# Token mixing of the first batch by groups of two head pairs instead of pair by pair, in a fused block-sparse attention and mixer kernel

## The chip, the core and the metric

The kernel runs on one core of a Trainium2 chip. A core has a matrix engine (TensorE, PE in the profile; its weight loads are shown apart as PEld), a vector engine (VectorE, DVE), a scalar engine (ScalarE, ACT), GpSimd (POOL) and SyncE (SP), each with its own program, and 16 DMA engines. Matmuls write to PSUM, and DVE or ACT bring the results to SBUF. The metric is the time of one execution on the device in microseconds, as a median of several; lower is better.

## The reference

Four batches, eight heads, 768 positions, 64 channels a head. Attention sees only some 32 x 32 blocks: the diagonal band, the first and last block row and column, and three sampled blocks for each block row. Its output, with the heads side by side as 512 channels, goes through a mixer: token mixing along the 768 positions, then channel mixing along the 512 channels.

```python
scores = scale * np.matmul(q, k.transpose(0, 1, 3, 2))          # mask: band, edges, sampled blocks
scores = np.where(mask, scores, -1000000000.0)
attn = np.exp(scores - max); attn = attn / (sum + 1e-09)
x = np.matmul(attn, v)              # then (batch, position, 8 heads * 64 channels)

xt = x.transpose(0, 2, 1)
h = np.maximum(xt @ w_tok1, 0.0) @ w_tok2     # 768 -> 256 -> 768, along positions
u = x + h.transpose(0, 2, 1)
h2 = np.maximum(u @ w_ch1, 0.0) @ w_ch2       # 512 -> 1536 -> 512, along channels
return u + h2
```

Token mixing treats each of the 512 channels by itself. So it can be done for any part of the channels as soon as the heads of that part are through attention. Channel mixing needs all 512 channels of a batch.

## The kernel before

The kernel works on 16 pairs of heads, four pairs to a batch. For each pair there are nine steps: a scores product on PE into a PSUM tile `ps`, an exponential on ACT into `et`, for later pairs a multiplication by the mask on DVE, and a product with V on PE into `po`, which DVE normalises into `x`. Token mixing takes `x` through `pm_tok` and `a_t`, adds to `x`, and transposes it into `uT`. Channel mixing (`pm_ch`, `rc`, `o`) reads `uT`.

All instructions are put in order when the program is built. A planner holds streams of PE instructions with priorities (the lower the number, the sooner) and lists of operations for the other engines, estimates when their inputs are ready, and at each step emits the first that is ready. Each engine then executes its instructions in the order in which they were emitted; the planner's estimates only shape this order.

```python
if self.now < self.tight:                      # the first 40 us of the plan
    t += 300.0 if 1.5 < s[0] < 2.5 else 100.0 if s[0] == 1 else 0.0
if t <= self.now: ... emit()
# ACT and DVE operations: of those that are ready, the one with the lowest (prio, number);
if eng == "act" and prio > 0 and self.exp_pending:
    continue                                   # ACT leaves other work while an exponential is due
```

The arrival of loads is an estimate as well. Loads are issued by GpSimd in the order V of pair 0; K, Q, V of pair 1; of pair 2; the two token weights; K, Q, V of pair 3; and so on.

```python
dma = {"free": 7.95 * US, "n": 0}
RATE = 200.0
LATE = (0, 290, 350, 0, 0, 190, 40, 700, 0)

def landing(issue, nbytes):
    late = LATE[dma["n"]] if dma["n"] < len(LATE) else 0
    dma["n"] += 1
    dma["free"] = max(dma["free"] + late, issue + 3.2 * US) + nbytes / RATE
    return Ev(dma["free"] + 0.15 * US)
```

K and Q of pairs 1 to 3 are transposed on PE straight from the landed rows, two slots of one head per transpose, without a relayout on DVE. This is so before and after the change:

```python
if raw is None:
    rows = lays[nm][:, c, :, :].rearrange("p h d -> p (h d)")       # pairs 4 to 7: after a relayout
else:
    lo = 2 * (c % 3)                                                 # pairs 1 to 3: the landed rows
    rows = raw[:, c // 3, lo : lo + 2, :].rearrange("p c d -> p (c d)")
```

Batches 1 to 3 do their token mixing by groups of two pairs (`tok`): products of 256 columns, and the transpose to `uT` by DMA. Batch 0 does it pair by pair (`tok_first`): products of 128 columns, and the transpose on PE. Its line numbers in the profile are L913 (first product), L936 (second), L945 (addition), L959 (transpose), L971 (copy); those of `tok` are L857, L882, L890.

```python
def tok_first(p):                              # p: pair 0 to 3 of batch 0
    g, lo = p // 2, 128 * (p % 2)
    urgent = 0.5 if p < 3 else -1
    deps = [x_there[p, h] for h in range(3)] + [tok1_there]
    # 2 x 6 matmuls: pm[128, 2, 128] += w_tok1 tile * x[:, g, sc, lo : lo + 128]
    # relu on DVE or ACT: a_t[:, :, 0:128] = max(pm, 0), priority `urgent`
    # twice: 6 matmuls into pm[128, 3, 128], then on DVE  x += pm  (128 x 384), priority `urgent`
    # 6 transposes of 128 x 128 into one PSUM tile, then one copy (128 x 768) to uT

P.stream(0, qk_stream())                       # scores
P.stream(1, pv_stream())                       # values
P.stream(TRP, tr_stream())                     # TRP = 2: transposes of K and Q
P.stream(TOKP, tok_first_stream(range(3)))     # TOKP = 0.7: token mixing of pairs 0 to 2
P.stream(-1, tok_first_stream((3,)))           # of pair 3, ahead of everything
P.stream(3, tok_stream((1, 2, 3)))             # of batches 1 to 3, by groups
P.stream(4, ch_stream())                       # channel mixing
```

Channel mixing goes over 12 x 2 tiles with four products each, one for each pair's part of `uT`, and the fourth needs pair 3 of the batch:

```python
yield 162.5, [st[b]["uT_there"][dmc], ch1_there[dmc]], tags, emit, ...   # dmc = 0 .. 3
```

Of the kernel before, what the change touches and what calls it, by code (L numbers as in the profile page):

```python
# [8 lines left out]
FP32 = mybir.dt.float32  # L9
BF16 = mybir.dt.bfloat16  # L10
# [4 lines left out]
ALU = mybir.AluOpType  # L15
# [159 lines left out]
def kernel(  # L175
# [12 lines left out]
    nc = tc.nc  # L188
# [3 lines left out]
    NC = 6  # L192
# [5 lines left out]
    NET = 7  # L198
    NPE = 8
    NT0 = 4  # L200
    TOKP = 0.7
    TRP = 2

    sb1 = ctx.enter_context(tc.tile_pool(name="sb1", bufs=1))
    sbw = ctx.enter_context(tc.tile_pool(name="sbw", bufs=2))
    psS = ctx.enter_context(tc.tile_pool(name="psS", bufs=2, space=bass.MemoryType.PSUM))
    psO = ctx.enter_context(tc.tile_pool(name="psO", bufs=1, space=bass.MemoryType.PSUM))
    psM = ctx.enter_context(tc.tile_pool(name="psM", bufs=3, space=bass.MemoryType.PSUM))
    ctx.enter_context(tc.manual_schedule())

    w_tok1 = sb1.tile([128, NC, DT], BF16, name="w_tok1")
    w_tok2 = sb1.tile([128, 2, 128, NC], BF16, name="w_tok2")
    w_ch1 = sb1.tile([128, 4, DC], BF16, name="w_ch1")
    w_ch2 = sb1.tile([128, 12, DM], BF16, name="w_ch2")
    ident = sb1.tile([128, 128], BF16, name="ident")
# [3 lines left out]
    P = Planner({"ps": 2, "po": 1, "pm": 3, "et": NET, "a_t": 2, "o": 3, "rc": 2,  # L219
                 "uT": 3})  # L220
    US = 1e3


    raws, arrive = {}, {}
    dma = {"free": 7.95 * US, "n": 0}
    RATE = 200.0
    LATE = (0, 290, 350, 0, 0, 190, 40, 700, 0)

    def landing(issue, nbytes):
        late = LATE[dma["n"]] if dma["n"] < len(LATE) else 0  # L230
        dma["n"] += 1
        dma["free"] = max(dma["free"] + late, issue + 3.2 * US) + nbytes / RATE
        return Ev(dma["free"] + 0.15 * US)


# [55 lines left out]
    tok1_there, tok2_raw = Ev(), Ev()  # L291
# [34 lines left out]
    for i in range(8):  # L326
# [5 lines left out]
        out=ind[R, :, :], in_=free(one[R, 0:1], 0, [[0, NC], [0, 128]]), compare_op=ALU.is_ge,  # L332
# [3 lines left out]
        out=ind[R, :, :], in_=ind[R, :, :], compare_op=ALU.is_ge, fill=0.0,  # L336
# [3 lines left out]
        out=ident[:, :], in_=free(one[:, 0:1], 0, [[0, 128]]), compare_op=ALU.is_equal, fill=0.0,  # L340
# [21 lines left out]
        out=edge[R, :], in0=edge[R, :], scalar1=-11.5, scalar2=None, op0=ALU.add  # L362
# [3 lines left out]
        out=edge[R, :], in0=edge[R, :], scalar1=121.0, scalar2=None, op0=ALU.is_gt  # L366
    )
    nc.vector.tensor_scalar(
        out=bandg[R, :], in0=dkf[R, :], scalar1=1.0, scalar2=edge[R, 0:1],
# [299 lines left out]
    def alias(a, b):  # L669
        a.same_as = b  # L670
# [4 lines left out]
    xs, x_there, po_of = {}, {}, {}  # L675
# [138 lines left out]
    def relu_op(o, i, deps, prio):  # L814
        n = i.free_size()

        def emit(eng):
            if eng == "act":
                nc.scalar.activation(out=o(), in_=i, func=AF.Relu)  # L819
            else:  # L820
                nc.vector.tensor_scalar(  # L821
                    out=o(), in0=i, scalar1=0.0, scalar2=None, op0=ALU.max
                )

        return P.op(("dve", "act"), {"dve": dve_psum(n), "act": act_cost(n)}, deps, emit, prio=prio)

    def new_uT(b):
        P.take("uT", st[b]["uT_rel"])
        st[b]["uT"] = sbw.tile([128, 2, NC, 2, 128], BF16, tag="uT", bufs=3, name=f"uT{b}")

    def turn_by_crossbar(b, g, u_evs):
        def emit(eng):
            if g == 0:
                new_uT(b)
            nc.sync.dma_start_transpose(
                out=st[b]["uT"][:, g, :, :, :].rearrange("e c m p -> e (c m) p"),
                in_=st[b]["u"][:, g, :, :].rearrange("p c e -> p (c e)"),
            )

        ev = P.op(("sp",), {"sp": 1600.0}, u_evs, emit, prio=2, lat=4000.0,  # L840
                  tags=[("uT", 1)] if g == 0 else [])
        for dmc in (2 * g, 2 * g + 1):
            alias(st[b]["uT_there"][dmc], ev)

    def tok(b, g):
        deps = [x_there[2 * g + 4 * b + i, h] for i in range(2) for h in range(3)] + [tok1_there]

        urgent = 3
        box = {}
        last, rel = Ev(), Ev()  # L850
        for t in range(2):
# [44 lines left out]
            alias(rel, ev)  # L896
            u_evs.append(ev)
        alias(a_rel, last)
        turn_by_crossbar(b, g, u_evs)

    def tok_first(p):
        g, lo = p // 2, 128 * (p % 2)
        urgent = 0.5 if p < 3 else -1
        box, last, rel = {}, Ev(), Ev()
        deps = [x_there[p, h] for h in range(3)] + [tok1_there]
        yield lambda: 0 in xs
        for t in range(2):
            for sc in range(NC):
                def emit(t=t, sc=sc):
                    if t == 0 and sc == 0:  # L910
                        P.take("pm", rel)
                        box["pm"] = psM.tile([128, 2, 128], FP32, tag="pm", name=f"pm_tok1_0_{p}")
                    nc.tensor.matmul(  # L913
                        out=box["pm"][:, t, :], lhsT=w_tok1[:, sc, 128 * t : 128 * t + 128],
                        rhs=xs[0][:, g, sc, lo : lo + 128],
                        start=(t == 0 and sc == 0), stop=(t == 1 and sc == NC - 1),
                    )
                begin = t == 0 and sc == 0
                yield 56.0, deps, [("pm", 1), ("a_t", 1)] if begin else [], emit, last if t == 1 and sc == NC - 1 else None
        if 0 not in st:  # L920
            st[0] = dict(u=xs[0], uT_there=[Ev() for _ in range(4)], uT_rel=Ev())
        a_rel = Ev()
        P.take("a_t", a_rel)
        a_t = sbw.tile([128, 2, 256], BF16, tag="a_t", name=f"a_t0_{p}")
        a_there = relu_op(lambda: a_t[:, :, 0:128], box["pm"][:, :, :], [last], urgent)
        alias(rel, a_there)
        u_evs = []
        for s3 in range(2):
            last, rel, ubox = Ev(), Ev(), {}
            for i in range(3):  # L930
                for t in range(2):
                    def emit(i=i, t=t, s3=s3, rel=rel, ubox=ubox):
                        if i == 0 and t == 0:
                            P.take("pm", rel)
                            ubox["pm"] = psM.tile([128, 3, 128], FP32, tag="pm", name=f"pm_tok2_0_{p}_{s3}")
                        nc.tensor.matmul(  # L936
                            out=ubox["pm"][:, i, :], lhsT=w_tok2[:, t, :, 3 * s3 + i],
                            rhs=a_t[:, t, 0:128], start=(i == 0 and t == 0), stop=(i == 2 and t == 1),
                        )
                    begin = i == 0 and t == 0  # L940
                    yield 56.0, [a_there, tok2_raw], [("pm", 1)] if begin else [], emit, last if i == 2 and t == 1 else None

            def add(eng, s3=s3, ubox=ubox):
                u = xs[0][:, g, 3 * s3 : 3 * s3 + 3, lo : lo + 128]
                nc.vector.tensor_tensor(out=u, in0=ubox["pm"][:, :, :], in1=u, op=ALU.add)  # L945

            ev = P.op(("dve",), {"dve": 556.0}, [last], add, prio=urgent)
            alias(rel, ev)
            u_evs.append(ev)
        alias(a_rel, last)  # L950
        last, rel, tbox = Ev(), Ev(), {}
        for sc in range(NC):
            def emit(sc=sc, rel=rel, tbox=tbox):
                if sc == 0:
                    if p == 0:
                        new_uT(0)
                    P.take("pm", rel)
                    tbox["pt"] = psM.tile([128, NC, 128], BF16, tag="pm", name=f"pm_ut_0_{p}")
                nc.tensor.matmul(  # L959
                    out=tbox["pt"][:, sc, :], lhsT=xs[0][:, g, sc, lo : lo + 128],  # L960
                    rhs=ident[:, :], start=(sc == 0), stop=(sc == NC - 1), is_transpose=True,
                )
            tags = [("pm", 1)] if sc == 0 else []
            if sc == 0 and p == 0:
                tags.append(("uT", 1))
            yield 56.0, [u_evs[sc // 3]], tags, emit, last if sc == NC - 1 else None

        def evac(eng, tbox=tbox):
            o, i = st[0]["uT"][:, g, :, p % 2, :], tbox["pt"][:, :, :]
            copy = nc.scalar.copy if eng == "act" else nc.vector.tensor_copy  # L970
            copy(out=o, in_=i)  # L971

        ev = P.op(("dve", "act"), {"dve": 555.0, "act": 740.0}, [last], evac, prio=urgent)
        alias(rel, ev)
        alias(st[0]["uT_there"][p], ev)

    def ch(b, pool, tag):
        yield lambda: b in st
# [77 lines left out]
    def tr_stream():  # L1056
        for p in range(NP):
            yield from transposes(p)

    def tok_stream(bs):  # L1060
        for b in bs:
            for g in range(2):
                yield from tok(b, g)

    def tok_first_stream(ps):
        for p in ps:
            yield from tok_first(p)

    def ch_stream():
        for b in range(B):  # L1070
            yield from ch(b, psM, "pm")

    P.stream(0, qk_stream())
    P.stream(1, pv_stream())
    P.stream(TRP, tr_stream())
    P.stream(TOKP, tok_first_stream(range(3)))
    P.stream(-1, tok_first_stream((3,)))
    P.stream(3, tok_stream((1, 2, 3)))
    P.stream(4, ch_stream())
    P.stream(1.8, mask_stream())  # L1080
# [78 lines left out]
```

## Time and profile before

| | before |
|---|---|
| time, median of 3 | 255.49 us (255.35 to 255.6) |
| span of the profiled execution | 253.6 us |
| PE busy | 246.9 us (97%), 2805 matmuls |
| PEld busy | 159.9 us (63%) |
| DVE busy | 179.4 us (71%) |
| ACT busy | 174.5 us (69%), 144 exponentials of 1022 ns |
| POOL busy | 49.5 us (20%) |
| first exponential starts, last starts | 7.4 us, 190.3 us |

All times within the profile count from the start of the span. A group of instructions is written as its line, engine, operation, output and inputs, shapes and count, then busy time and mean of one, then the idle time of the engine just before such instructions and what ended it. In the chain of waits each piece is work that the end of the program depended on. Matmuls are pipelined: the time that one takes from start to end is longer than the distance to the next, so runs of them show their rate better than single ones.

### The profile page before, as it was taken

The page shows a single profiled execution, that of the slowest core. Times are in us where ns is not written, and L with a number is a line of the kernel's source. Part 1 is how long each engine was busy: PE and PEld are TensorE (multiplying, and loading weights), DVE is VectorE, ACT ScalarE, POOL GpSimd, SP SyncE. Part 2 cuts the span into 40 slices and gives each one's busy share as a digit, 9 for nine tenths or more (in the row PEclk, how much of TensorE's full clock was granted, in tenths as well). Part 3 has the DMA queues.
Part 4 walks back from the last instruction along what each step waited for, and adds up shares of the span by engine and source line. Part 5 has one row for each costly group of instructions (what it writes and reads, how often), then busy time and mean ns, then how long its engine had stood idle before and what let it go on. Part 6 is the DMA issues. An engine that isn't in the chain of part 4 may idle for free.

```text
span 253.6 us, 6679 instructions
## 1 busy us (share of the span) xinstructions
PE 246.9 (97%) x2805; PEld 159.9 (63%) x2805; DVE 179.4 (71%) x394; ACT 174.5 (69%) x216; POOL 49.5 (20%) x84
## 2 busy tenths in 40 slices
PE   8889999999999999999999999999999999999994
PEld 3679998755666556656676566567567644566444
DVE  7784978998998988899889898988885312200222
ACT  5899999788888577778888777677786510277000
POOL 8746979477400000000000000000000000000000
PEclk9999999999999999999999999999999999999999
DMA  6999999999955926254032212311400212300122
GB/s 146 185 218 202 212 203 205 203 201 201 201 80 128 162 82 92 48 136 106 3 72 56 62 44 42 105 44 44 103 3 1 53 53 84 124 3 0 41 115 94
DMA packets 42462, 26.36 MB, mean 104 GB/s; under 512 B 23680, under 2 KB 38800, under 8 KB 42432
## 3 DMA queue, kind: packets, MB, share of 16 engines
q0 software_dynamic: 15104, 12.98, 32.4%
q1 hardware_dynamic: 27056, 12.76, 20.6%
q8 instruction: 22, 0.36, 0.6%
q10 hardware_dynamic: 272, 0.20, 0.3%
q14 instruction: 8, 0.07, 0.1%
HBM read 26.74 MB, written 6.29 MB: 130 GB/s over the span
## 4 chain that ended last, share of the span: by engine, by line
PE 92%; ACT 4%; DVE 2%; issue 1%
PE pm_ch L994 25%; PE pm_ch L1020 25%; PE ps L691 16%; PE po L777 14%; ACT et L701 3%; PE pm_tok L882 3%; PE pm_tok L857 3%; PE ps_idle L321 2%; PE pm_tok L913 1%; PE tk L633 1%; PE pm_tok L936 1%; PE tq L633 1%; DVE et L709 0%; DVE qtb L422 0%; DVE qtb L662 0%
## 5 line engine op out<-in xcount | busy, mean ns | idle before, releaser
L701 ACT ACTIVATE et<-ps 128x1024 bf16<-128x1024 f32 x144 | 139.2, 1022 | 32.1 <-PE ps L691 31.3
L994 PE MATMUL pm_ch<-uT,w_ch 128*128 128x384 bf16 x384 | 72.6, 326 | 0.1
L709 DVE TENSOR_TENSOR et<-et,mask 128x1024 bf16<-128x1024 bf16 x108 | 70.3, 683 | 1.2 <-ACT et L701 1.2
L1020 PE MATMUL pm_ch<-w_ch,rc 128*128 128x512 bf16 (+2 forms) x312 | 70.8, 363 | 0.0
L777 PEld LDWEIGHTS <-et 128*128 128x128 bf16 x1152 | 47.6, 97 | 16.5 <-issue 3.4
L691 PE MATMUL ps<-qtb,ktb 64*128 64x256 bf16 (+1 forms) x576 | 54.6, 272 | 2.2 <-ACT et L701 2.1
L777 PE MATMUL po<-vaug,et 128*128 128x65 bf16 x1152 | 54.3, 193 | 0.2 <-DVE et L709 0.2
L994 PEld LDWEIGHTS <-w_ch 128*128 128x128 bf16 x384 | 34.3, 97 | 20.7 <-issue 2.7
L819 ACT ACTIVATE rc<-pm_ch 128x384 bf16<-128x384 f32 x58 | 28.5, 492 | 24.3 <-PE pm_ch L994 24.2
L1032 DVE TENSOR_TENSOR o<-pm_ch,x 128x512 f32<-128x512 f32 x23 | 15.8, 688 | 41.5 <-PE pm_ch L1020 41.5
L1020 PEld LDWEIGHTS <-rc 128*128 128x128 bf16 x312 | 27.3, 97 | 24.4 <-issue 1.9
L691 PEld LDWEIGHTS <-ktb 64*128 64x128 bf16 (+1 forms) x576 | 29.0, 95 | 21.5 <-issue 16.7
L821 DVE TENSOR_SCALAR rc<-pm_ch 128x384 bf16<-128x384 f32 x38 | 21.1, 555 | 7.1 <-PE pm_ch L994 6.6
L792 DVE TENSOR_TENSOR x<-po,recip 128x256 bf16<-128x256 f32 x48 | 20.4, 424 | 1.7
L791 DVE RECIPROCAL recip<-po 128x4 f32<-128x4 f32 x48 | 8.6, 180 | 10.0 <-PE po L777 9.8
L890 DVE TENSOR_TENSOR x<-pm_tok,x 128x512 bf16<-128x512 f32 x18 | 11.8, 684 | 2.4 <-PE pm_tok L882 2.4
L882 PE MATMUL pm_tok<-a_t,w_tok 128*128 128x256 bf16 x72 | 10.0, 275 | 0.0
L857 PE MATMUL pm_tok<-x,w_tok 128*128 128x256 bf16 x72 | 9.2, 273 | 0.0
L882 PEld LDWEIGHTS <-w_tok 128*128 128x128 bf16 x72 | 7.5, 127 | 0.6 <-issue 0.2
L259 POOL DMA_DIRECT2D vraw<-in_v_dram x10 | 7.4, 737 | 2.3 <-DVE qtb L662 1.0
L537 POOL COPY mask<-maskb 128x240 bf16<-128x240 bf16 (+1 forms) x18 | 7.4, 491 | 0.0
L259 POOL DMA_DIRECT2D kraw<-in_k_dram x9 | 6.7, 742 | 3.8 <-PE pm_tok L913 1.4
(104 smaller groups left out, 133.9 us busy)
## 6 DMA issues: line engine op xcount, KB each, us to landing
out_dram<-o SPq DMA_DIRECT2D x23, 256.0 KB, 2.0
w_ch<-in_moe_w_ch_dram POOLq DMA_DIRECT2D x8, 384.0 KB, 10.2
vraw<-in_v_dram POOLq DMA_DIRECT2D x10, 192.0 KB, 7.6
kraw<-in_k_dram POOLq DMA_DIRECT2D x9, 192.0 KB, 8.2
qraw<-in_q_dram POOLq DMA_DIRECT2D x9, 192.0 KB, 7.8
w_tok<-in_moe_w_tok_dram POOLq DMA_DIRECT2D x2, 384.0 KB, 10.2
ktb<-in_v_dram POOLq DMA_DIRECT2D x3, 192.0 KB, 7.3
kf<-in_k_dram SPq DMA_DIRECT2D x2, 192.0 KB, 3.2
```

The source lines that it names most:

```text
L691: nc.tensor.matmul(out=ps[:, hd, 256 * i : 256 * i + 256], lhsT=ktb[n][rows, h, 256 * jj + 128 * i : 256 * jj + 128 * i + 128], rhs=qtb[n] ...
L701: nc.scalar.activation(out=et[:, :, :], in_=ps[:, :, :], func=AF.Exp, scale=0.125)
L709: nc.vector.tensor_tensor(out=ets[s][:, :, :].rearrange("k h (i q) -> k h i q", i=2), in0=ets[s][:, :, :].rearrange("k h (i q) -> k h i q" ...
L777: nc.tensor.matmul(out=po[:, hd, c, :], lhsT=et[:, hd, 256 * i + 128 * c : 256 * i + 128 * c + 128], rhs=va[:, hd, 2 * jj + i, 0:65], star ...
L792: nc.vector.tensor_tensor(out=free(xs[b][:, pb // 2, 2 * t, 128 * (pb % 2) : 128 * (pb % 2) + 128], 0, [[64, 2], [256, 2], [1, 64]],), in0 ...
L819: nc.scalar.activation(out=o(), in_=i, func=AF.Relu)
L821: nc.vector.tensor_scalar(out=o(), in0=i, scalar1=0.0, scalar2=None, op0=ALU.max)
L857: nc.tensor.matmul(out=box["pm"][:, t, :], lhsT=w_tok1[:, sc, 128 * t : 128 * t + 128], rhs=xs[b][:, g, sc, :], start=(t == 0 and sc == 0) ...
L882: nc.tensor.matmul(out=ubox["pm"][:, i, :], lhsT=w_tok2[:, t, :, 2 * s2 + i], rhs=a_t[:, t, :], start=(i == 0 and t == 0), stop=(i == 1 an ...
L994: nc.tensor.matmul(out=pbox["pm"][:, 0:384], lhsT=w_ch1[:, dmc, 128 * cc : 128 * cc + 128], rhs=st[b]["uT"][:, dmc // 2, 3 * sh : 3 * sh + ...
L1020: nc.tensor.matmul(out=pbox["pm"][:, 0:n], lhsT=box["rc"][:, cc, 128 * sc : 128 * sc + 128], rhs=w_ch2[:, cc, lo : lo + n], start=(cc == 0 ...
L1032: nc.vector.tensor_tensor(out=o[:, :].rearrange("p (g e) -> p g e", g=2), in0=pbox["pm"][:, :].rearrange("p (g e) -> p g e", g=2), in1=st[ ...
```

## The change

Token mixing of batch 0 goes by groups of two pairs, like that of the other batches, in place of pair by pair. `tok_first` and its two streams go. `tok` serves batch 0 as well, in a stream of priority 0.5, with operations on DVE and ACT of priority 0.5; a group starts when both of its pairs are normalised. The transposes of batch 0 stay on PE, six for each pair, now after the three additions of the group; the other batches keep the DMA transpose. The group form has half as many matmuls, each of twice the columns. In the same edit the estimates of the loads' arrival are set back to a start of 7.6 us, without delays of single loads. The change is named for the transposes of K and Q from the landed rows, but these are in both kernels and the diff doesn't touch them.

```diff
-    TOKP = 0.7
-    TRP = 2
...
-    dma = {"free": 7.95 * US, "n": 0}
+    dma = {"free": 7.6 * US}
     RATE = 200.0
-    LATE = (0, 290, 350, 0, 0, 190, 40, 700, 0)
 
     def landing(issue, nbytes):
-        late = LATE[dma["n"]] if dma["n"] < len(LATE) else 0
-        dma["n"] += 1
-        dma["free"] = max(dma["free"] + late, issue + 3.2 * US) + nbytes / RATE
+        dma["free"] = max(dma["free"], issue + 3.2 * US) + nbytes / RATE
         return Ev(dma["free"] + 0.15 * US)
...
     def tok(b, g):
         deps = [x_there[2 * g + 4 * b + i, h] for i in range(2) for h in range(3)] + [tok1_there]
 
-        urgent = 3
+        urgent = 0.5 if b == 0 else 3
...
-        turn_by_crossbar(b, g, u_evs)
-
-    def tok_first(p):
-        ...                                    # all of tok_first goes
+        if b > 0:
+            turn_by_crossbar(b, g, u_evs)
+            return
+        for dmc in (2 * g, 2 * g + 1):
+            ...                                # per pair: six transposes and a copy, as in tok_first
+                yield 56.0, [u_evs[sc // 2]], tags, emit, last if sc == NC - 1 else None
+            ...
+            ev = P.op(("dve", "act"), {"dve": 555.0, "act": 740.0}, [last], evac, prio=urgent)
...
-    P.stream(TRP, tr_stream())
-    P.stream(TOKP, tok_first_stream(range(3)))
-    P.stream(-1, tok_first_stream((3,)))
+    P.stream(2, tr_stream())
+    P.stream(0.5, tok_stream((0,)))
     P.stream(3, tok_stream((1, 2, 3)))
```

More of the change, by code (lines that the diff above doesn't have):

```diff
@@ L898, in tok @@
         alias(a_rel, last)
-        turn_by_crossbar(b, g, u_evs)
-    def tok_first(p):
[L902 to L907, printed above, removed]
+        if b > 0:
+            turn_by_crossbar(b, g, u_evs)
+            return
+        for dmc in (2 * g, 2 * g + 1):
+            last, rel, tbox = Ev(), Ev(), {}
@@ L908, in tok_first, with emit @@
             for sc in range(NC):
-                def emit(t=t, sc=sc):
-                    if t == 0 and sc == 0:
+                def emit(sc=sc, dmc=dmc, rel=rel, tbox=tbox):
+                    if sc == 0:
+                        if dmc == 0:
+                            new_uT(b)
                         P.take("pm", rel)
-                        box["pm"] = psM.tile([128, 2, 128], FP32, tag="pm", name=f"pm_tok1_0_{p}")
+                        tbox["pt"] = psM.tile([128, NC, 128], BF16, tag="pm", name=f"pm_ut_{b}_{dmc}")
@@ L913, in emit @@
                     nc.tensor.matmul(
-                        out=box["pm"][:, t, :], lhsT=w_tok1[:, sc, 128 * t : 128 * t + 128],
-                        rhs=xs[0][:, g, sc, lo : lo + 128],
-                        start=(t == 0 and sc == 0), stop=(t == 1 and sc == NC - 1),
-                    )
[L918 to L947, printed above, removed]
-            alias(rel, ev)
-            u_evs.append(ev)
@@ L950, in tok_first @@
[L950 to L975, printed above, removed]
+                        out=tbox["pt"][:, sc, :],
+                        lhsT=st[b]["u"][:, g, sc, 128 * (dmc % 2) : 128 * (dmc % 2) + 128],
@@ new lines, in emit, with evac @@
+                        rhs=ident[:, :], start=(sc == 0), stop=(sc == NC - 1), is_transpose=True,
+                    )
+                tags = [("pm", 1)] if sc == 0 else []
+                if sc == 0 and dmc == 0:
+                    tags.append(("uT", 1))
+                yield 56.0, [u_evs[sc // 2]], tags, emit, last if sc == NC - 1 else None
+            def evac(eng, dmc=dmc, tbox=tbox):
+                o, i = st[b]["uT"][:, g, :, dmc % 2, :], tbox["pt"][:, :, :]
+                if eng == "act":
+                    nc.scalar.copy(out=o, in_=i)
+                else:
+                    nc.vector.tensor_copy(out=o, in_=i)
@@ L977, in ch @@
+            ev = P.op(("dve", "act"), {"dve": 555.0, "act": 740.0}, [last], evac, prio=urgent)
+            alias(rel, ev)
+            alias(st[b]["uT_there"][dmc], ev)
     def ch(b, pool, tag):
@@ L1063, in tok_stream @@
                 yield from tok(b, g)
-    def tok_first_stream(ps):
-        for p in ps:
-            yield from tok_first(p)
     def ch_stream():
```

## The prediction

> **What bounds the kernel now.** I read the page's 40 slices first, then the busy time of each engine by stretch, then the chain that ended last, and last the timeline from 7 to 54 us, where all that is changed lies.
>
> In the busy time by stretch the columns after the colon are the stretch's length and then PE, PEld, DVE, ACT and POOL busy us with their instruction counts:
>
> ```profile
> core 0: us, PE busy (x) PEld busy (x) DVE busy (x) ACT busy (x) POOL busy (x), PEclk, DMA share, GB/s
> 18.00:44.00 26.00, 24.72 (x417) 23.04 (x417) 19.74 (x49) 25.46 (x27) 20.71 (x38) 1.00 1.23 205
> ```
> ```profile
> 44.00:53.00 9.00, 8.65 (x150) 6.48 (x147) 8.60 (x21) 7.09 (x9) 4.89 (x8) 1.00 1.27 203
> ```
> ```profile
> 60.00:80.00 20.00, 20.00 (x256) 13.40 (x255) 18.30 (x41) 17.65 (x23) 5.39 (x8) 1.00 0.93 152
> ```
>
> There are three stages. From 18 to 44 us ACT is the bound: its 27 exponentials fill 25.46 of 26 us, one every 0.963 us (26/27). From about 53 us to the end PE has no gap at all, so there every microsecond of PE work left over is a microsecond of time. Between the two is a hand-over in which neither is full: ACT 7.09 of 9 us. It ends when channel mixing of batch 0 can start, because only that gives PE as much work as it can take. The chain through the hand-over (start, us, what):
>
> ```profile
> 47.57 0.84 PE pm_tok L913 x12
> 48.41 0.02 issue
> 48.44 0.42 DVE a_t L821
> 48.86 0.60 DVE et L709
> 49.46 0.02 DVE x L945
> 49.48 0.44 issue
> 49.92 0.55 DVE x L945
> 50.47 0.60 DVE et L709
> 51.07 0.51 DVE uT L971
> 51.58 0.04 issue
> 51.62 0.49 PE pm_ch L994 x2
> ```
>
> This is token mixing of the last pair of batch 0, alone: first product (L913), ReLU (a_t), second product with its two additions (x L945), transpose and copy (uT), and at 51.62 the first channel product that needs all four pairs. The pair's last attention block was normalised by 47.02 (start 46.59 plus 0.43, in the timeline), so the chain takes 4.60 us. The other three pairs have gone through the same steps beside the exponentials, from 19.5, 28.5 and 39.0 us on.
>
> **What the Trainium skill says.** "TensorE: Matmul & The Clock Gate", section "Back-to-back issue gap", gives N/2.4 + 2.5 ns between warm matmuls, an estimate of 55.8 ns for 128 columns and 109 for 256, and about 81 ns in a sustained stream at 128 columns. The trace agrees with the formula, not with the 81: the run of 12 above lasts 0.83 us with a last matmul of 0.219, so (0.83 - 0.219)/11 = 55.5 ns; a run of 12 with 256 columns counts 1.31 us in the chain, 109 ns each. The same page's opening table gives VectorE and ScalarE a strict first-in first-out queue, and lets TensorE pull only weight loads ahead. The trace agrees for PE: at 17.70 us one weight load for L691 is done, and its matmul comes only at 19.07, after 1.18 us of idle PE. "Perfetto Trace Analysis", section "Identifying the Most-Contended Engine", says that matmul busy time is no measure of headroom. That holds here too (PE 20.00 of 20 us busy, PEld 13.40), so below I count PE work by the intervals just derived.
>
> **Part 1: PE work that leaves the ACT-bound stage.** Per pair, before: 12 + 12 products of 128 columns and 6 transposes, 30 x 55.5 ns = 1.67 us. After, for a group of two pairs: 12 + 12 products of 256 columns and 12 transposes, 24 x 109 + 12 x 55.5 = 3.28 us. The batch costs 6.67 us before and 6.56 us after: PE work hardly changes, -0.1 us. What changes is when it is done. Before, three pairs (5.0 us) were done before 44 us; after, the group of pairs 0 and 1 alone (3.3 us) can be, since the second group needs pair 3. In that stage PE was nearly full: 27 exponentials need 27 x (436 + 236 ns, the costs that the kernel's own planner gives to one scores and one values step; the trace's L691 and L777 runs bear them out) = 18.1 us, 42 transposes 2.3, token mixing 5.0, together 25.4 of 26 us. Without pair 2's mixing PE idles about 1.7 us more there, since it has nothing else ready and ACT sets the pace. The work reappears after 44 us, where nothing hides it: **+1.7 - 0.1 = +1.6 us**.
>
> **Part 2: the hand-over gets longer.** These durations are from the groups of instructions by line and shape:
>
> ```profile
> L819 ACT ACTIVATE a_t<-pm_tok 128x512 bf16<-128x512 f32 x5 | 3.0, 597 | 1.4 <-PE pm_tok L857 1.3
> ...
> L821 DVE TENSOR_SCALAR a_t<-pm_tok 128x512 bf16<-128x512 f32 x1 | 0.7, 691 | 0.0
> ```
> ```profile
> L890 DVE TENSOR_TENSOR x<-pm_tok,x 128x512 bf16<-128x512 f32 x18 | 11.8, 684 | 2.4 <-PE pm_tok L882 2.4
> ```
>
> Starting where it starts now (47.6): first product 11 x 109 + 272 (its last matmul) = 1.47 us, to 49.05; ReLU on 512 elements 0.69, to 49.8; the first third of the second product 3 x 109 + 272 = 0.6, to 50.4; three additions of 0.684 on DVE, which outlast the matmuls, to 52.5; the last eight transposes, 8 x 55.5 + 0.16, to 53.1; two copies of 0.556 on one engine, the second ending near 54.0. So channel mixing is complete in its inputs at about 54.0 instead of 51.6, 2.4 us later. PE has in that time its steps of attention, held by ACT to two steps per 2.6 us (exponential pairs start at 44.89, 47.43, 50.17, 52.53): 0.54 + 16 x 0.03 = 1.0 us of PE in 2.6. In 44.4 to 53.3 I count 8.2 us of PE work in 8.9 (0.7 idle). In a hand-over of about 10.5 us there would be 4.1 of attention, 0.5 of values steps in arrears, 1.0 of transposes and 3.3 of mixing, 8.9 us, so 1.6 idle: **+0.9 us**. Part 1 has already counted the extra mixing as moved here.
>
> **Part 3: the landing estimates.** They move no transfer; they set the order in which instructions are put on each engine, and a wrong order stalls engines that can't step aside. GpSimd's load issues wait for earlier loads, and so show when these landed:
>
> ```profile
> 12.02 0.71 POOL L259 DMA_DIRECT2D qraw<-in_q_dram  x1 [0.75 <-DMA qraw<-in_q_dram]
> 13.02 0.71 POOL L259 DMA_DIRECT2D vraw<-in_v_dram  x1 [0.29 <-DMA vraw<-in_v_dram]
> ...
> 18.83 0.71 POOL L259 DMA_DIRECT2D kraw<-in_k_dram  x1 [1.27 <-DMA w_tok<-in_moe_w_tok_dram]
> ```
>
> Q of pair 1 landed by 12.02, V by 13.02, the first token weights by 18.83. The estimates before, each load adding 196,608 bytes / 200 = 983 ns, plus the listed delays, say 11.68, 12.67 and 18.5; those after say 10.70, 11.68 and 16.6, so 1.3 to 2.2 us too early. The copy of V of pair 1 on DVE and the transposes of pairs 2 and 3 would then be put ahead of work that is ready. Much of it is absorbed: scores come first on PE, the planner adds 0.3 us to transposes before 40 us, and the trace itself runs some tenths behind the plan. Nor are the token weights needed early any more, since the first group starts only near 28 us. I take a third of the 1.3 us error as lost exponentials, a choice and not a reading: **+0.4 us**. Against it, DVE and PE have less to do between the exponentials, and ACT has 0.54 us idle in 18 to 44 us (26 - 25.46), of which at most **-0.4 us** could come back.
>
> **Sum.** 1.6 + 0.9 + 0.4 - 0.4 = +2.5 us on 255.49. Since the first group may run a little ahead of pair 3's work and close some of the gap in the hand-over, I lower it by 0.2 and predict 257.8 us, +0.9%.
>
> **Rivals.** (a) *The order doesn't matter, only the sum of PE work.* If PE is the bound from start to end, as its 97% on the page suggests, the time falls by the 0.1 us of part 1, and perhaps a little more through 48 fewer weight loads: about 255.4. For it speaks that PE never shows a whole idle slice; against it that ACT sets the pace until 44 us. (b) *The early stalls dominate.* If the landing estimates put PE or DVE in front of a late load at each of pairs 1, 2 and 3, exponentials would be lost about 1 us at a time, in a stage where nothing makes up for it: +3 us from this alone, and a time near 260.5. For it speaks that ACT already loses 1.3 us between 16.7 and 18.0 us, with good estimates, behind copies of K and Q (0.5 waiting, 0.8 in a copy of its own); against it the margins named above. (c) *A better packing.* Pair-wise mixing takes one of three buffers for products in PSUM 16 times (4 pairs, each one, two and one), the groups take 12 (2 groups, each one, three and two), and in before the last chain goes ahead of scores. Fewer interruptions could give ACT back its gaps in the hand-over (1.9 us of 9 are idle): at best -1.9 + 1.6 + 0.4, so again near 255.6. Against it, the gaps there are followed by PE's scores, not by buffers.
>
> **Range and chances.** Rivals (a) and (c) put the lower end at 255.5; I take 255.7, since both need ACT to stay the pace-maker and yet cost nothing. Part 3 at its full 1.3 us and a hand-over with 1 us more of idle make 257.8 + 0.9 + 1.0 = 259.7; with a little of (b), 260.2. Two per cent are 5.1 us: 260.6 is reached only in rival (b), for which I give 0.07; below 250.4 nothing I see can lead, 0.01. The rest, 0.92, is within 2%.
>
> **What would show it.** In the changed profile: L857 and L882 with 96 matmuls each and no 128-column products; the first channel product that needs all four pairs at about 54 us plus any early delay; PE idle, counted by intervals, up by about 1.7 us in 18 to 44 us; exponentials there still every 0.96 us; then PE without gaps and the end later by the sum. Part 3 is right in kind if DVE or PE waits for loads of pairs 1 to 3 that it doesn't wait for now. I am wrong if the channel products start no later than 52 us, if ACT gains in the hand-over what PE loses, or if the delay is already there at 18 us, which would be rival (b).

## The result, and the profile after

| | before | after |
|---|---|---|
| time, median | 255.46 us (255.35 to 255.6) | 256.5 us (256.26 to 256.92) |
| after over before | | 1.0042, 95% interval 1.0025 to 1.006 |
| 36th exponential starts | 43.17 us | 42.96 us |
| first channel product with all four pairs | 51.62 us | 55.43 us |
| transposes of K and Q (of 84) done by 44.0 us | 66 | 76 |

The change costs 1.04 us, 0.4%. The profiled execution of the changed kernel was its longest, 256.92 us, so its trace (span 255.2 us) is 1.6 us longer than the one of before (253.6), more than the medians differ.

Busy time by stretch in the changed kernel, with the columns as before (length, then PE, PEld, DVE, ACT, POOL, each with its count):

```profile
18.00:44.00 26.00, 25.11 (x398) 22.51 (x396) 20.39 (x47) 25.26 (x27) 20.83 (x38) 1.00 1.23 205
```
```profile
44.00:53.00 9.00, 8.52 (x140) 6.50 (x137) 8.08 (x17) 7.68 (x9) 5.17 (x8) 1.00 1.28 203
53.00:56.00 3.00, 2.62 (x37) 1.51 (x35) 2.97 (x8) 2.63 (x3) 1.95 (x4) 1.00 1.31 201
...
60.00:80.00 20.00, 20.00 (x239) 13.08 (x237) 18.30 (x41) 16.82 (x22) 5.59 (x8) 1.00 1.08 161
```

The line from 53 to 56 us of the kernel before, for comparison:

```profile
53.00:56.00 3.00, 3.00 (x44) 1.93 (x43) 2.90 (x6) 2.70 (x4) 2.20 (x4) 1.00 1.31 203
```

The three stages are the same. From 18 to 44 us ACT still has its 27 exponentials. What is new stands in the line from 53 to 56: PE, without a gap there before, is idle 0.38 us of 3 even by busy time, and the hand-over now ends after 55 us. From 60 to 240 us PE has no gap in either kernel.

The chain through the hand-over of the changed kernel (start, us, what):

```profile
46.05 0.04 DVE x L787
46.09 0.30 issue
46.39 0.35 DVE vaug L562
46.74 1.80 DVE et L704 x3
48.55 0.60 DVE a_t L816
49.15 0.10 DVE recip L786
49.25 0.02 issue
49.27 0.04 DVE x L787
49.31 0.31 issue
49.62 0.68 DVE et L704
50.30 1.20 DVE x L885 x2
51.50 1.20 DVE et L704 x2
52.70 0.60 DVE x L885
53.30 0.10 DVE recip L786
53.40 0.02 issue
53.42 0.04 DVE x L787
53.46 0.31 issue
53.77 0.68 DVE et L704
54.45 0.94 DVE uT L921 x2
55.39 0.04 issue
55.43 0.48 PE pm_ch L944 x2
```

The group's mixing steps (a_t, three x L885, two uT) are there as counted. But before and between them stand seven maskings of exponentials (et L704; 1.80 + 0.68 + 1.20 + 0.68 = 4.36 us), which have nothing to do with mixing; DVE does them where its program has them. In the shorter chain of before there were two (0.60 each). Not all of the seven cost time: during the first three PE was still busy with the first product.

```profile
47.16 1.05 PE L852 MATMUL pm_tok<-x,w_tok 128*128 128x256 bf16 x8
48.46 0.68 DVE L816 TENSOR_SCALAR a_t<-pm_tok 128x512 bf16<-128x512 f32 x1
```

That product ends at 48.21 us and its ReLU starts 0.25 us later. The four maskings after the ReLU (2.56 us) are those that stretch the chain. From the last normalisation (46.05 + 0.42) to the first full channel product it takes 8.96 us, before 4.60.

To say where time is lost, busy time is too coarse. So I add up the **matmul work** done by a moment, each matmul at the distance to the next in an unbroken run of its kind: 30 ns for a product with V, 109 or 68 for scores (88 or 64 rows), 55.5 for a transpose or a product of 128 columns, 109, 162.5 and 216 for 256, 384 and 512. These come from runs in the chain of before (96 matmuls L994 in 15.60 us, 72 of L1020 in 15.54, 16 of L777 in 0.49, 8 of L691 in 0.54). Without the 12 products of constants at the start (L321) both kernels add up to some 232.4 us, the changed one to 0.1 less, so work missing at any moment against the kernel before has to be made up later. The traces' first exponential lies between 7.0 and 7.9 us, so all are aligned there. In us, against the kernel before (a negative number is a lead; 28.6 us is near the start of the first group's mixing):

| kernel | missing by 28.6 | by 44 | more from 44 to 60 | more from 60 to 220 | time over before |
|---|---|---|---|---|---|
| the changed kernel | 0.41 | 0.45 | 1.08 | -0.08 | 1.0042 |
| c2 groups, estimates + 0.1 us | 0.73 | 0.33 | 1.10 | -0.08 | 1.0043 |
| e2 groups, estimates of before | 1.16 | 1.20 | 0.62 | -0.08 | 1.0061 |
| e4 groups, second group first | 0.90 | 0.50 | 0.55 | 0.32 | 1.0067 |
| e5 groups, transposes held | 1.02 | 1.29 | 0.53 | 0.21 | 1.0069 |
| c1 pairs, estimates + 0.1 us | 0.35 | 0.34 | 0.00 | 0.00 | 1.0009 |
| e3 pairs, last not first | 0.33 | 0.30 | 0.20 | 1.00 | 1.0066 |
| e7 pairs, late start of channels | 0.00 | -0.10 | 1.67 | 0.48 | 1.0077 |
| e9 pairs, estimates of after, DVE | 0.39 | 0.29 | -0.06 | 0.95 | 1.0018 |
| e1b pairs, estimates of after | -0.86 | -1.25 | 0.29 | not read | 1.0009 |
| e6 group, then pairs | 1.01 | 1.32 | 0.04 | not read | 1.0135 |
| e8 pairs, then group | 0.01 | -0.02 | 0.93 | not read | 1.0068 |

In the last three traces some per cent of the matmul records after 80 us are missing, so that column is left out. The columns "by" carry the error of the alignment: c1, whose time is that of before, has 0.34 there; the columns "from" don't. The loss of the changed kernel is complete by 60 us: 0.45 in the ACT-bound stage, little more than that error, and 1.08 in the hand-over. c2, whose profiled execution is at its median, has 0.33 and 1.10. What is missing at 60 us are channel products, 2.21 us of them; scores and products with V are 0.78 us ahead.

### The profile page after: what moved, and what is told of

Same layout as the page of the kernel before. It is cut to its first block, busy times and chain, and to the rows that moved or that the text cites. A ratio compares the mean times of both kernels' runs of the same rounds, so it can differ in the third digit from the quotient of the medians.

```text
span 255.2 us, 6567 instructions
## 1 busy us (share of the span) xinstructions
PE 247.9 (97%) x2757; PEld 159.3 (62%) x2757; DVE 179.7 (70%) x390; ACT 174.1 (68%) x216; POOL 49.7 (19%) x84
## 4 chain that ended last, share of the span: by engine, by line
PE 84%; DVE 5%; DMA 3%; POOL 3%; ACT 2%; issue 1%; ACTq 0%
PE pm_ch L970 25%; PE pm_ch L944 25%; PE ps L686 14%; PE po L772 13%; PE pm_tok L877 4%; PE pm_tok L852 4%; DMA vraw<-in_v_dram 3%; ACT et L696 2%; DVE et L704 2%; DVE x L885 1%; DVE vaug L562 1%; POOL vraw L254 1%; POOL kraw L254 1%; DVE x L787 1%; POOL qraw L254 1%
## 5 line engine op out<-in xcount | busy, mean ns | idle before, releaser
L704 DVE TENSOR_TENSOR et<-et,mask 128x1024 bf16<-128x1024 bf16 x108 | 70.1, 683 | 0.5 <-ACT et L696 0.4
L814 ACT ACTIVATE rc<-pm_ch 128x384 bf16<-128x384 f32 x60 | 29.5, 492 | 25.0 <-PE pm_ch L944 24.8
L816 DVE TENSOR_SCALAR rc<-pm_ch 128x384 bf16<-128x384 f32 x36 | 19.9, 554 | 7.0 <-PE pm_ch L944 6.7
L885 DVE TENSOR_TENSOR x<-pm_tok,x 128x512 bf16<-128x512 f32 x24 | 15.8, 685 | 1.9 <-PE pm_tok L877 1.8
L877 PE MATMUL pm_tok<-a_t,w_tok 128*128 128x256 bf16 x96 | 14.1, 276 | 0.1
L852 PE MATMUL pm_tok<-x,w_tok 128*128 128x256 bf16 x96 | 12.8, 273 | 0.0
L877 PEld LDWEIGHTS <-w_tok 128*128 128x128 bf16 x96 | 10.1, 127 | 1.6 <-issue 1.3
L852 PEld LDWEIGHTS <-w_tok 128*128 128x128 bf16 x96 | 8.6, 97 | 1.6 <-issue 0.6
## 6 DMA issues: line engine op xcount, KB each, us to landing
out_dram<-o SPq DMA_DIRECT2D x23, 256.0 KB, 2.0
```

The source lines that it names most:

```text
L704: nc.vector.tensor_tensor(out=ets[s][:, :, :].rearrange("k h (i q) -> k h i q", i=2), in0=ets[s][:, :, :].rearrange("k h (i q) -> k h i q" ...
L816: nc.vector.tensor_scalar(out=o(), in0=i, scalar1=0.0, scalar2=None, op0=ALU.max)
L852: nc.tensor.matmul(out=box["pm"][:, t, :], lhsT=w_tok1[:, sc, 128 * t : 128 * t + 128], rhs=xs[b][:, g, sc, :], start=(t == 0 and sc == 0) ...
L877: nc.tensor.matmul(out=ubox["pm"][:, i, :], lhsT=w_tok2[:, t, :, 2 * s2 + i], rhs=a_t[:, t, :], start=(i == 0 and t == 0), stop=(i == 1 an ...
L885: nc.vector.tensor_tensor(out=st[b]["u"][:, g, 2 * s2 : 2 * s2 + 2, :], in0=ubox["pm"][:, :, :], in1=xs[b][:, g, 2 * s2 : 2 * s2 + 2, :], ...
```

## The experiments

Several explanations were put to the test. Theory A: the time is lost in the hand-over, because batch 0's channel mixing starts later. Theory B: it is lost before 30 us, because the order follows wrong estimates of arrival. Later came M (mixing moved out of the ACT-bound stage cost little because other work took its place) and C (any change re-deals the order, and bubbles come and go).

**The estimates alone (e1, e1b).** The kernel before with the changed kernel's estimates:

```diff
-    dma = {"free": 7.95 * US, "n": 0}          # and LATE
+    dma = {"free": 7.6 * US}
```

> The kernel before with one part of the change alone: the estimates of the loads' arrival of the changed kernel (start 7.6 us, no single delays); token mixing stays pair by pair. Theory A (the hand-over: batch 0's channel mixing starts later because the last mixing is a group of two pairs, and PE idles before it) gives this part nothing: 255.5 us, first full channel product at 51.6 us. Theory B (the order made from wrong estimates stalls PE and DVE behind loads before 30 us) gives it the whole loss: 256.5 us, with about 0.7 us less matmul work done by 28 us than in the kernel before. By the matmul work done up to each moment in the two traces I expect both in part: 255.9 us.

Measured: 255.87 us, ratio 1.0016 (0.9997 to 1.0036). Its profile was taken at a lower TensorE clock (0.987), so only that of the second run is read.

> The kernel before with the changed kernel's estimates of the loads' arrival once more, since the profile of the first look at it began with a lower TensorE clock. From its 22 times: 255.4 to 256.3 us, median near 255.7; if the estimates matter by themselves, up to 0.5 us of matmul work is missing by 20 us; if they don't, the profile agrees with that of the kernel before within 0.3 us throughout.

Measured: 255.88 us, ratio 1.0009 (0.9985 to 1.0034). Neither form of the expectation came. Nothing is missing by 20 us, and the profile doesn't agree with that of before within 0.3 us: by 44 us it is 1.25 us ahead in work, with the 36th exponential at 42.13 in place of 43.17 us. The first full channel product comes at 51.77 all the same. At 60 us 0.96 us of the lead are left, and what becomes of it can't be followed, since records are missing later; the median time is no shorter. The estimates alone have no effect on the time that can be told from none, and the whole loss of 1.04 us lies outside both intervals; B falls for pairs.

**Groups with the estimates of before (e2).** The reverse combination.

```diff
-    dma = {"free": 7.6 * US}
+    dma = {"free": 7.95 * US, "n": 0}          # and LATE, in the changed kernel
```

> The changed kernel with the kernel before's estimates of the loads' arrival; token mixing of batch 0 by groups. Theory A: the loss stays, 256.5 us, and the first full channel product near 55 us. Theory B: the loss goes, 255.5 us. In part, as the work done in the traces says (about 0.9 us lost between 53 and 56 us, 0.7 before 28 us): 256.1 us.

Measured: 257.03 us, ratio 1.0061 (1.0031 to 1.0091). The loss stays, if anything larger. So, as far as these intervals tell, the loss hangs on the form of the mixing and not on the estimates. More of it lies before 44 us here than in the changed kernel (1.20 against 0.45), less after. In the same aligned count, 70 of the 84 transposes of K and Q are done by 44 us here, in the changed kernel all 84; the 14 are 0.8 us of work, as much as the difference. B falls for groups too: with the estimates of before, 1.16 us are missing by 28.6 us.

**Pairs, the last not ahead (e3).**

```diff
-        urgent = 0.5 if p < 3 else -1
+        urgent = 0.5
-    P.stream(TOKP, tok_first_stream(range(3)))
-    P.stream(-1, tok_first_stream((3,)))
+    P.stream(TOKP, tok_first_stream(range(4)))
```

> The kernel before, pair by pair, but the last pair's chain in the same stream as the others (priority 0.7 on PE, 0.5 on DVE and ACT) and not ahead of the scores. Theory A in the form 'the length of the chain of the last mixing counts, whatever makes it long': first full channel product 0.5 to 1.5 us later than 51.6, time +0.3 us, 255.8. In the form 'only the group's size counts': 255.5.

Measured: 256.9 us, ratio 1.0066 (1.004 to 1.0092), more than any theory said. The first full channel product moves to 52.58 us, but only 0.20 us of work goes missing in the hand-over. Most of the rest goes later, at batch 1's token mixing near 77 us, far from the edit:

```profile
76.81 0.42 PE L777 MATMUL po<-vaug,et 128*128 128x65 bf16 x8
77.44 0.60 PE L882 MATMUL pm_tok<-a_t,w_tok 128*128 128x256 bf16 x4 [0.22 <-DVE x L890]
77.97 0.39 PE L691 MATMUL ps<-qtb,ktb 64*128 64x256 bf16 x4
78.69 0.39 PE L691 MATMUL ps<-qtb,ktb 64*128 64x256 bf16 x4 [0.33 <-ACT et L701]
```

The second product's last third waits for an addition that frees its PSUM tile, and the scores behind it start late and then wait for an exponential. Such a bubble is what C means. The time of e3 therefore can't be used for or against A; its work in the hand-over can.

**Groups, the second ahead of everything (e4).**

```diff
-    P.stream(0.5, tok_stream((0,)))
+    P.stream(0.5, tok(0, 0))
+    P.stream(-1, tok(0, 1))                    # and priority -1 on DVE and ACT
```

> The changed kernel with the second group's mixing ahead of everything (PE, DVE and ACT priority -1), as the last pair's chain is in the kernel before. Theory A with priority as the cause of the later start: first full channel product moves from 55.4 to about 53.5 us and the time from 256.5 to 256.0. If the group's own length is the cause (three additions of 0.68 us, two copies): the start moves by less than 0.7 us and the time stays at 256.4 or so. Theory B: no change, 256.5.

Measured: 256.82 us, ratio 1.0067 (1.0041 to 1.0093). The start moves to 53.04 us and the loss in the hand-over halves, 1.08 to 0.55, as A expects of a start 2.4 us sooner. But neither the time nor the sum of the missing work falls to match: 0.32 us more goes missing after 60 us. The expected 256.0 is missed.

**Controls (c1, c2).** The estimates' start moved by 0.1 us, in the kernel before and in the changed one.

```diff
-    dma = {"free": 7.95 * US, "n": 0}          # c2: 7.6
+    dma = {"free": 8.05 * US, "n": 0}          # c2: 7.7
```

> A control: the kernel before with nothing changed but the start of the arrival estimates, 8.05 us in place of 7.95. No theory of mixing or loads gives this 0.1 us any effect beyond 0.1 us: 255.5. A third theory, C (any change re-deals the order of thousands of instructions, and single bubbles of half a microsecond to one come and go), expects a shift of up to 1 us in either direction, more likely up, since the kernel before was chosen among such orders.

> The same control on the changed kernel: the start of the estimates 7.7 us in place of 7.6. Theory A and B: 256.5 us, as the changed kernel. Theory C: anywhere from 255.7 to 257.3.

Measured: c1 255.56 us, ratio 1.0009 (0.997 to 1.0048); c2 256.82 us, ratio 1.0043 (1.0015 to 1.0071). Neither moves, as far as these intervals tell (c1's reaches from -0.8 to +1.2 us). C isn't needed for the changed kernel, whose loss comes back with another order before 28 us (0.73 missing there in place of 0.41) and the same sum.

**Transposes held (e5).**

```diff
+                if p == 6:
+                    deps.append(qk_done[3])    # in the changed kernel
```

> The changed kernel with the 12 transposes of K and Q of pair 6 held until all scores of pair 3 are issued (near 43 us), so that they can't fill PE in the stage in which ACT is the bound. In the changed kernel 80 of these 84 transposes were done by 44 us, in the kernel before 66. Theory M (moving mixing out of that stage cost little because transposes moved in): with 12 transposes, 0.67 us, moved out again, the time rises by 0.6 us over the changed kernel's 256.5, to 257.1. Rival (the idle PE of the hand-over takes up whatever is moved there): no change, 256.5.

Measured: 257.53 us, ratio 1.0069 (1.0049 to 1.0089), so 0.7 us over c2 of the same set, though the intervals overlap. The transposes' PE time by stretch, first tk, then tq, in the changed kernel:

```profile
18.00:44.00 26.00, 2.91 (x30) 2.74 (x5) 0.00 (x0) 1.00 1.23 205
```
```profile
18.00:44.00 26.00, 2.23 (x26) 3.67 (x7) 1.00 1.23 205
```

and in e5:

```profile
18.00:44.00 26.00, 2.50 (x24) 2.20 (x4) 0.00 (x0) 1.00 1.23 205
```
```profile
18.00:44.00 26.00, 1.94 (x23) 2.99 (x6) 0.00 (x0) 1.00 1.23 205
```

The counts after PE's time add up to 56 and 47; before the change they were 24 and 18, 42. (With the 24 done before 18 us, the changed kernel has started 80 of the 84 by 44.0 us, as the expectation has it, and ended 76, as the table has it.) In the aligned count, 69 are done in e5 and 84 in the changed kernel. With these 15, 0.84 us, out of the ACT-bound stage, 1.29 us of work is missing by 44 us in place of 0.45, which is just 0.84 more: M. Of the 0.84 us, 0.55 comes back in the hand-over (0.53 lost there in place of 1.08), as the rival said. Both hold in part.

**The start alone (e7).** The kernel before, the last pair's copy to uT put behind a later masking.

```diff
+        if p == 3:
+            ev = P.op(("dve",), {"dve": 555.0}, [last, et_there[4, 2, 1]], evac, prio=urgent)
```

> The kernel before, pair by pair with the last pair first, with one thing added: the copy of the last pair to uT is put after the masking of the 44th exponential, so that channel mixing of batch 0 starts near 55.5 us, as in the changed kernel, instead of 51.6. Nothing else is changed. Theory A (the later start alone costs the time, PE having too little else): about 0.9 to 1.1 us more, 256.5, with the loss of matmul work between 51 and 56 us. If the start as such is harmless (other work fills in and comes off later): 255.6.

Measured: 257.84 us, ratio 1.0077 (1.0053 to 1.0101). The first full channel product comes at 55.81 us. PE in the hand-over:

```profile
52.28 0.39 PE L691 MATMUL ps<-qtb,ktb 64*128 64x256 bf16 x4 [0.30 <-ACT et L701]
52.61 0.80 PE L777 MATMUL po<-vaug,et 128*128 128x65 bf16 x16
53.59 0.42 PE L777 MATMUL po<-vaug,et 128*128 128x65 bf16 x8 [0.19 <-DVE et L709]
53.94 0.61 PE L691 MATMUL ps<-qtb,ktb 64*128 64x256 bf16 x8
54.75 0.42 PE L777 MATMUL po<-vaug,et 128*128 128x65 bf16 x8 [0.20 <-DVE x L792]
55.34 0.41 PE L777 MATMUL po<-vaug,et 128*128 128x65 bf16 x8 [0.18 <-DVE et L709]
55.81 0.81 PE L997 MATMUL pm_ch<-uT,w_ch 128*128 128x384 bf16 x4
```

PE has only attention left, and waits again and again for exponentials, maskings and a normalisation. A later start by 4.2 us (55.81 - 51.62) loses 1.67 us of work, 0.4 us for each; some 0.5 us more goes at batch 1's mixing near 77 us, so that the time is longer than the 256.5 us expected. This shows A's mechanism with nothing else changed. The changed kernel starts nearly as late and loses less. From 44 to 60 us it has 2.21 us less of channel products than the kernel before and 1.12 us more of other work, e7 2.55 less and 0.86 more. Its mixing is work for PE in that time (24 products of 109 ns in place of 24 of 55.5, and 12 transposes in place of 6, 1.61 us more), though 0.97 us of transposes of K and Q are done already. This is an account of the work; no run tested it.

**Half and half (e6, e8).** With `tok` and `tok_first` side by side, estimates of before:

```diff
+    P.stream(0.5, tok(0, 0)); P.stream(0.7, tok_first(2)); P.stream(-1, tok_first(3))    # e6
+    P.stream(0.7, first_two()); P.stream(0.5, tok(0, 1))         # e8: pairs 0, 1, then the group
```

> The kernel before, but pairs 0 and 1 of batch 0 mixed as a group; pairs 2 and 3 stay pair by pair, the last ahead of everything; estimates as in the kernel before. So pair 2's mixing stays in the stage in which ACT is the bound and the last chain stays short. If only what happens to pairs 2 and 3 counts: 255.5 us, first full channel product near 51.6, and no matmul work lost between 44 and 60 us. If the group form itself costs (wider steps beside the exponentials): up to 0.7 us of work missing by 44 us, and 256.1.

> The mirror image: pairs 0 and 1 pair by pair, pairs 2 and 3 as a group, not ahead of the scores; estimates as in the kernel before. If only what happens to pairs 2 and 3 counts, all of the loss is here: 256.5 to 257.0 us, first full channel product near 55 us, about 1 us of matmul work lost between 44 and 60 us. If the loss needs the first group too: 255.8.

Measured: e8 257.41 us, ratio 1.0068 (1.0046 to 1.0091); e6 258.87 us, ratio 1.0135 (1.0087 to 1.0184). e8 goes nearly as expected up to 60 us: nothing missing by 44 us, 0.93 in the hand-over, the first full channel product at 53.97 us and not near 55; its time is 0.4 us above the range. It shows M again: the mixing of pair 2, 1.66 us, is not done by 44 us, but 12 more transposes of K and Q, 25 products with V and 4 of scores are, 1.7 us together. e6 misses both numbers, by far. The stretch from 18 to 28 us, in e6 and then in e8:

```profile
18.00:28.00 10.00, 8.45 (x136) 7.22 (x135) 6.11 (x19) 9.97 (x12) 7.15 (x13) 1.00 1.30 204
```
```profile
18.00:28.00 10.00, 9.03 (x154) 8.46 (x154) 6.26 (x18) 9.84 (x11) 6.33 (x12) 1.00 1.29 203
```

As long as the first group waits for pair 1, PE lacks pair 0's mixing: 136 matmuls in place of 154. Then group, pair 2 and pair 3 crowd together, with pair 2's products at 42 us (39 us before), and the first full channel product comes at 54.27 us. So in e6 the first group matters as well, by the work that it keeps back until 28 us. The 1.36 us missing by 60 us don't explain a time 3.5 us longer; where the rest goes is open, since the trace lacks records there.

**An attempt at a better version (e9).** e1 with the last pair's ReLU and copy on DVE only.

```diff
-        a_there = relu_op(...)                 # for p == 3: on DVE alone
-        ev = P.op(("dve", "act"), ...)         # for p == 3: ("dve",)
```

> An attempt at a version that beats both: the kernel before with the changed kernel's estimates of arrival, in whose last trace the 36th exponential came 1.0 us sooner than in the kernel before, but where the last pair's ReLU and copy to uT went to ACT, behind exponentials, and the first full channel product came at 51.8 us all the same, 6.3 us after the last normalisation in place of 4.6. Here these two are kept on DVE. If the length of that chain counts: first full channel product 50.0 to 51.0 us and 0.3 to 0.8 us less than the same kernel without it, 255.2 us, near or below the kernel before. If not, 255.9.

Measured: 255.94 us, ratio 1.0018 (1.0001 to 1.0035). No gain. The first full channel product comes at 52.14 us and not between 50 and 51, so this run doesn't tell what a shorter chain would be worth. About 1 us of work goes missing between 100 and 140 us, 0.64 us of it in one stretch from 112.3 us. None of these kernels beats the kernel before.

## Why the prediction was right or wrong

The direction and the stages were right, and 256.5 us lies in the range. The size was wrong, +2.3 us predicted and +1.04 measured, and of the two places where the loss was expected one showed little of it.

**Part 1 failed**, at the sentence "Without pair 2's mixing PE idles about 1.7 us more there, since it has nothing else ready". Of the +1.6 us, 0.45 shows in the trace. PE did have work ready: transposes of pairs 6 and 7, which in the kernel before came at 44.9 to 47.0 us, after the scores of pair 3. The trace of before showed them there, and in the changed kernel they stand earlier:

```profile
44.94 0.51 PE L633 MATMUL tq<-ident,qlay 128*128 128x128 bf16 x6
46.17 0.50 PE L633 MATMUL tk<-ident,klay 128*128 128x128 bf16 x6
46.51 0.50 PE L633 MATMUL tq<-ident,qlay 128*128 128x128 bf16 x6
```
```profile
39.84 0.50 PE L628 MATMUL tq<-ident,qlay 128*128 128x128 bf16 x6
43.59 0.50 PE L628 MATMUL tk<-ident,klay 128*128 128x128 bf16 x6
43.92 0.50 PE L628 MATMUL tq<-ident,qlay 128*128 128x128 bf16 x6
```

In the aligned count by 44 us (in the changed trace 0.22 us later, by when all 84 are done) the changed kernel has 1.38 us less token mixing and 0.33 less of its transposes, but 18 more transposes of K and Q (1.00 us) and 0.30 us more products with V; the sum is the 0.4 us missing. e5 takes 15 of the 18 out again, and the missing work goes up to 1.29. In e2, where 14 of them stay late by themselves, it is 1.20. So "nothing else ready" was the wrong step, and how much of the ready work moves up depends on the order that the planner makes.

**Part 2** had the mechanism, which e7 shows by itself, but its size, +0.9 predicted and 1.08 measured, is luck. The count behind it was wrong: by the prediction's own intervals PE has 7.5 us of work from 44.4 to 53.3 us in the trace of before (scores 2.2, products with V 1.7, transposes of K and Q 1.0, mixing 1.7, channel products 1.0), not 8.2. So 1.4 us were idle and not 0.7, and a step to 1.6 would have been +0.2. On the other side, the 1.0 us of transposes that it put into the new hand-over were done before it, and the start came at 55.43 us and not at 54.0. The ReLU was done sooner than predicted, at 49.14 in place of 49.8 us; from there to the end of the second copy it took 6.24 us in place of 4.2, with the four maskings that the prediction had left out. What stands in between changes with the order: e2 has two maskings on its chain from 48 us on, besides scores and products with V, and starts at 54.86.

**Part 3** was a choice of +0.4 us. The stalls it named are in the trace:

```profile
10.23 0.51 PE L628 MATMUL tk<-ident,kraw 128*128 128x128 bf16 x6 [0.90 <-DMA kraw<-in_k_dram]
...
15.73 0.36 DVE L562 COPY vaug<-vraw 128x768 bf16<-128x768 bf16 x1 [0.86 <-DMA vraw<-in_v_dram]
```

PE stands 0.90 us before the K of pair 1, DVE 0.86 before a V. But by 20.6 us only 0.03 us of work is missing, and e1 puts the whole effect of the estimates on pairs within -0.1 and +0.9 us (interval), e1b within -0.4 and +0.9, so the +0.4 is neither confirmed nor excluded. The exponentials that start the next pair come no later: the tenth starts at 17.78 us, before the change at 18.00. The gain of at most 0.4 us set against it is there too, the 36th exponential 0.2 us sooner.

**The rivals.** (a), that order doesn't matter, falls with e7: the same work with one copy put later costs 2 us. (b) falls with e1. (c) falls too, though the sign named for it, ACT gaining in the hand-over what PE loses, did appear: the 45th exponential starts at 53.95 us in place of 55.15. That gave no time back; the last one starts hardly sooner, 189.94 against 190.28, since PE is the bound by then. (After 240 us PE has gaps again, 3.1 us before the change and 3.2 after; the prediction has none to the end.)

## What to carry to other kernels

Where one engine sets the pace and another has gaps, taking work out of the gaps costs only what no other ready work can fill. So list what is ready there, and where the trace has it now, before charging the moved work in full. At the hand-over from one bound to the next, count the chain with the other work that stands between its steps on the same engine. And with an order made by a planner, compare the work done by each moment and not the end alone: a small edit can lose a microsecond far away from itself, as e3 and e9 did.

## What the runs showed that was not expected

An arrangement that was ahead by 1.25 us of matmul work at 44 us and by 0.96 at 60 (e1b) has a median time no shorter than the kernel before; why is open. Wrong estimates of arrival put PE in front of a load for 0.90 us without the next pair coming later: ACT's stretch without exponentials between the first two pairs, 16.7 to 18.0 us before the change, is shorter after it, and the second pair's begin 0.2 us sooner. And halving the loss in the hand-over (e4) gave no time back; where its remaining 0.3 us after 60 us go wasn't followed further.
